# Six products into two PSUM banks: in turn, or three into one and then three into the other

## The chip, the cores and the metric

The kernel runs on one core of a Trainium2 chip. The metric is device time in microseconds (us) of one execution. The runs of the kernel before took 2927.8, 2927.21 and 2923.53 us; their median is 2927.21 us. One more execution was profiled. It took 2925.64 us and its span, from the first to the last instruction, is 2923.9 us.

## The reference

The input `x` is 8 x 3072 x 256 in float32. Three things follow one another:

```python
X = np.fft.fft(np.fft.fft(x, axis=1), axis=2).real      # 24576 rows of 256
h = X @ w_in                                            # first layer, 256 -> 2048
y = (h - np.tanh(h)) @ w_out                            # its second product, 2048 -> 256
h2 = y @ w_in2                                          # second layer, 256 -> 1024
solu = h2 * softmax(h2)
out = layernorm(solu) * g_ln @ w_out2                   # 1024 -> 256
```

## The kernel before

The Fourier transform along the sequence comes first, in some 200 us, and leaves its result in DRAM. The transform along the features is folded into `w_in`. The rest of the run is one long loop over 48 blocks of 512 rows each, and in each block over 16 chunks `m` of 128 hidden features: 768 steps. What one step does on each engine:

- `ab` (L714 to L724) multiplies the step's part of `w_in` with the block's rows: six products of 256 columns on TensorE, into one PSUM bank.
- `lead` and `act_in` (L727 to L749): three VectorE operations make the hidden features h, and ScalarE takes their tanh.
- `act_out` (L752 to L763) forms g = h - tanh(h) on VectorE and splits it in two numbers of reduced precision (float32r), so that products lose nothing that matters: ScalarE rounds g to its high part (L152), and GpSimd then subtracts that from g and leaves the low part (L155). Both stand in one tile `gh`, of which there are three.
- `o1` (L765 to L795) is the second product of the first layer. It multiplies this step's `gh` with 128 rows of `w_out`, which are split in the same way. Three products make one: high by high, low weights by high `gh`, high weights by low `gh`. The 256 outputs are two halves `mt` of 128, each with a PSUM bank of its own (`x2_0` and `x2_1`, one buffer each), so a step has six products of 512 columns here. Over the 16 steps of a block, both banks add up. After the last one (`m == NM - 1`) ScalarE copies both banks to `x2f`, rounds them to `x2s`, and GpSimd makes their low parts.
- `layer2` (L919 to L944) does the second layer for the four groups of 128 rows of a block, spread over the steps in quarters: `h2` (six products of 512 columns into one bank, L806), `expo`, `soft`, `square`, `turn` (a transposition by way of DRAM, which SyncE's queue carries), `split_moved` (high and low parts `ut`, on ScalarE and GpSimd), and `outp` (twelve products of 256 columns, L896).

Nothing reorders the work: every engine runs its instructions in the order in which the program issues them (the schedule is written by hand), and waits at semaphores for the others. The main loop (L949 on) sets this order. In each step TensorE gets `ab`, then one product of the second layer or none, then `o1` of two steps before (four before, in the first block), then again one product of the second layer or none. GpSimd gets, in the order of issue, the low part of `gh` of the step before, the second layer's small operations and the low parts of `ut`, and after a block's last `o1` the low parts of `x2s`.

The order within `o1` is that of two loops, the outer over the three pairs of parts, the inner over the two banks:

```python
for i, (hw, hg) in enumerate(((0, 0), (1, 0), (0, 1))):   # part of the weights, part of gh
    for mt in range(2):                                   # bank
        nc.tensor.matmul(x2p[n][mt], wo1[c][:, hw, k, mt * P : (mt + 1) * P], gh[:, hg], ...)
```

So the six products go to banks 0, 1, 0, 1, 0, 1, and the first four read the high part of `gh`, the last two its low part.

Of the kernel before, what the change touches and what calls it, by code (L numbers as in the profile page):

```python
# [127 lines left out]
def fft2_moe_moe_kernel(  # L128
# [22 lines left out]
    def rnd(o, i):  # L151
        nc.scalar.activation(out=o, in_=i, func=AF.Copy)  # L152

    def rest(eng, o, i, hi):
        eng.tensor_tensor(out=o, in0=i, in1=hi.bitcast(F32), op=ALU.subtract)  # L155
# [609 lines left out]
    def o1(n, m):  # L765
        if m == 0:
            x2p[n] = [p_x2.tile([P, 2 * GP], F32, tag=f"x2_{mt}", name=f"x2p{n}_{mt}") for mt in range(2)]
        gh = gs.pop((n, m))
        c, k = divmod(m, 4)

        for i, (hw, hg) in enumerate(((0, 0), (1, 0), (0, 1))):
            for mt in range(2):
                nc.tensor.matmul(  # L773
                    x2p[n][mt],
                    wo1[c][:, hw, k, mt * P : (mt + 1) * P],
                    gh[:, hg],
                    start=(m == 0 and i == 0),
                    stop=(m == NM - 1 and i == 2),
                )
        if m == NM - 1:  # L780
            xs = wk.tile([P, 2, 2, 2 * GP], F32R, tag="x2s", name=f"x2s{n}")
            x2s[n] = xs
            if n == NG - 1:
                for mt, p in enumerate(x2p.pop(n)):
                    rnd(xs[:, 0, mt], p)
                    rest(nc.vector, xs[:, 1, mt], p, xs[:, 0, mt])
                return
            xf = wk.tile([P, 2, 2 * GP], F32, tag="stage", name=f"x2f{n}")
            for mt, p in enumerate(x2p.pop(n)):
                rnd(xf[:, mt], p)  # L790
            for mt in range(2):
                rnd(xs[:, 0, mt], xf[:, mt])
                rest(nc.gpsimd, xs[:, 1, mt], xf[:, mt], xs[:, 0, mt])
# [155 lines left out]
    for step in range(steps + 2):  # L949
# [13 lines left out]
        for s in (range(o1_done, min(s1 + 1, steps))):  # L963
            o1(*divmod(s, NM))
# [115 lines left out]
```

## Time and profile before

| | |
|---|---|
| median of three runs | 2927.21 us |
| profiled execution | 2925.64 us |
| its span | 2923.9 us |
| TensorE busy | 2881.3 us (99%) |
| VectorE busy | 2403.0 us (82%) |
| GpSimd busy | 1965.2 us (67%) |
| ScalarE busy | 1803.9 us (62%) |
| mean granted TensorE clock | 0.997 |
| HBM traffic | 103 GB/s over the span |

PE is TensorE's stream of products (MATMUL) and PEld its stream of weight loads (LDWEIGHTS), which runs beside it: each product has one load. DVE is VectorE, ACT is ScalarE, POOL is GpSimd. A row of a group of instructions names the line, the engine, the operation, output and inputs, their shapes and the count. A line can be that of a helper: L152 is every rounding on ScalarE, and L155 every subtraction that leaves a low part, so the tile's name tells which one it is. The starts of successive products lie closer together than their durations, because they are pipelined: what a product costs TensorE is read from start to start.

### The profile page before, as it was taken

What the parts mean: (1) busy time and instruction counts of PE and PEld (TensorE: products, weight loads), DVE (VectorE), ACT (ScalarE), POOL (GpSimd) and SP (SyncE); (2) the same over time, 40 slices, a digit from 0 to 9 for tenths busy, and PEclk for the clock granted to TensorE, in tenths of its full rate; (3) what the DMA queues carried; (4) which work ended last, traced back from release to release, by engine and by line L of the source; (5) the groups of instructions that cost most, each with busy time, mean ns of one, the idle gap of its engine ahead of it and who ended that gap; (6) DMA issues with size and microseconds to landing.
All of it is one profiled execution on the core that took longest, in us unless ns stands there. A gap on an engine that the chain in (4) does not pass through costs nothing. (4 is left out here: it accounts for less than half of the span.)

```text
span 2923.9 us, 49792 instructions
## 1 busy us (share of the span) xinstructions
PE 2881.3 (99%) x16799; PEld 2482.3 (85%) x16799; DVE 2403.0 (82%) x4818; ACT 1803.9 (62%) x3287; POOL 1965.2 (67%) x2413
## 2 busy tenths in 40 slices
PE   7899999999999999999999999999999999999999
PEld 3467888888888888888888888888888888888888
DVE  7897888888888888888888888888888888888885
ACT  2345666666666666666666666666666666666665
POOL 0156767777677776777777767777677766777763
PEclk9999999999999999999999999999999999999999
DMA  8781333343334334344334433443434443443331
GB/s 306 252 298 31 88 94 94 90 94 92 87 94 98 89 89 99 88 94 93 89 95 91 96 89 90 97 91 90 94 92 92 93 92 88 95 98 89 89 91 42
DMA packets 876512, 303.75 MB, mean 104 GB/s; under 512 B 788520, under 2 KB 837688, under 8 KB 872960
## 3 DMA queue, kind: packets, MB, share of 16 engines
q1 hardware_dynamic: 873536, 293.95, 40.9%
q10 hardware_dynamic: 2304, 6.29, 0.5%
q8 instruction: 132, 2.16, 0.3%
q14 instruction: 124, 1.02, 0.1%
q0 software_dynamic: 416, 0.33, 0.0%
HBM read 162.01 MB, written 138.47 MB: 103 GB/s over the span
## 5 line engine op out<-in xcount | busy, mean ns | idle before, releaser
L155 POOL TENSOR_TENSOR gh<-g,gh 128x512 fp32r<-128x512 f32 x768 | 993.2, 1297 | 469.3 <-ACT gh L152 469.3
L773 PE MATMUL x2p<-gh,wo 128*128 128x512 f32 x4608 | 1206.5, 397 | 3.6 <-POOL gh L155 2.3
L773 PEld LDWEIGHTS x2p<-gh,wo 128*128 128x128 f32 x4608 | 825.5, 189 | 166.3 <-POOL gh L155 10.7
L749 ACT ACTIVATE t<-h 128x512 f32<-128x512 f32 x768 | 459.5, 598 | 547.8 <-DVE h L743 446.3
L720 PEld LDWEIGHTS ab<-zs,wt 128*128 128x128 f32 x4608 | 649.0, 188 | 72.5 <-DVE h L743 2.7
L720 PE MATMUL ab<-zs,wt 128*128 128x256 f32 x4608 | 668.0, 280 | 2.1 <-DVE h L743 2.1
L754 DVE TENSOR_TENSOR g<-h,t 128x512 f32<-128x512 f32 x768 | 521.8, 679 | 172.0 <-ACT t L749 168.5
L152 ACT ACTIVATE gh<-g 128x512 fp32r<-128x512 f32 x768 | 480.9, 626 | 235.5 <-DVE g L754 223.1
L896 PE MATMUL po<-wo,ut 128*128 128x256 f32 x4608 | 597.8, 278 | 4.4 <-ACT ut L152 2.6
L806 PE MATMUL ph<-wi,x2s 128*128 128x512 f32 x2304 | 597.1, 394 | 0.0
L896 PEld LDWEIGHTS po<-wo,ut 128*128 128x128 f32 x4608 | 560.7, 188 | 10.1 <-POOL ut L155 5.0
L727 DVE SCALAR_TENSOR_TENSOR asb<-nb,wnu,ab 128x256 f32<-128x256 f32 x768 | 367.1, 478 | 221.1 <-PE ab L720 219.3
L806 PEld LDWEIGHTS ph<-wi,x2s 128*128 128x128 f32 x2304 | 420.0, 188 | 84.5
L155 POOL TENSOR_TENSOR ut<-um,ut 128x512 fp32r<-128x512 f32 x372 | 480.8, 1292 | 0.8 <-issue 0.8
L743 DVE TENSOR_TENSOR h<-asb,ab 128x256 f32<-128x256 f32 x768 | 328.8, 428 | 26.5
L742 DVE TENSOR_TENSOR h<-asb,ab 128x256 f32<-128x256 f32 x768 | 329.1, 429 | 26.2
L819 ACT ACTIVATE e<-ph,st 128x1024 f32<-128x1024 f32 x192 | 214.3, 1116 | 97.9 <-DVE st L817 82.1
L817 DVE TENSOR_REDUCE st<-ph 128x1 f32<-128x1024 f32 x192 | 233.6, 1216 | 3.5 <-PE ph L806 3.5
L825 DVE SCALAR_TENSOR_TENSOR u<-ph,e 128x1024 f32<-128x1024 f32 x192 | 233.6, 1217 | 0.0
L152 ACT ACTIVATE ut<-um 128x512 fp32r<-128x512 f32 x372 | 231.1, 621 | 0.0
L856 DVE STREAM_TRANSPOSE tb<-u 128x1024 f32<-128x1024 f32 x186 | 230.0, 1236 | 0.0
L836 ACT ACTIVATE e<-u,st 128x1024 f32<-128x1024 f32 x192 | 219.5, 1143 | 0.0
(101 smaller groups left out, 1531.2 us busy)
## 6 DMA issues: line engine op xcount, KB each, us to landing
mv_d<-tb SPq DMA_DIRECT2D x186, 512.0 KB, 2.6
um<-mv_d SPq DMA_DIRECT2D x744, 128.0 KB, 3.8
out<-o SPq DMA_DIRECT2D x192, 128.0 KB, 1.7
x<-xr SPq DMA_DIRECT2D x23, 1024.0 KB, 7.6
z_d<-zt SPq DMA_DIRECT2D x16, 384.0 KB, 7.4
z_d<-zt ACTq DMA_DIRECT2D x16, 384.0 KB, 6.6
wo<-w_out SPq DMA_DIRECT2D x24, 256.0 KB, 5.5
zf<-z_d SPq DMA_DIRECT2D x48, 128.0 KB, 3.3
```

The costliest lines, as they stand in the source:

```text
L152: nc.scalar.activation(out=o, in_=i, func=AF.Copy)
L155: eng.tensor_tensor(out=o, in0=i, in1=hi.bitcast(F32), op=ALU.subtract)
L720: nc.tensor.matmul(pab[:, u], wt[c][:, hw, u, o : o + P], zs[:, hz, u], start=(i == 0), stop=(i == 2))
L727: nc.vector.scalar_tensor_tensor(out=asb, in0=zg[n][1], scalar=wnu[:, m : m + 1], in1=pab[:, 0], op0=ALU.mult, op1=ALU.add)
L742: nc.vector.tensor_tensor(out=h[:, 0], in0=asb, in1=pab[:, 1], op=ALU.add)
L743: nc.vector.tensor_tensor(out=h[:, 1], in0=asb, in1=pab[:, 1], op=ALU.subtract)
L749: nc.scalar.activation(out=t, in_=h, func=AF.Tanh)
L754: nc.vector.tensor_tensor(out=g, in0=hs.pop((n, m)).rearrange("p u n -> p (u n)"), in1=ts_.pop((n, m)).rearrange("p u n -> p (u n)"), op=A ...
L773: nc.tensor.matmul(x2p[n][mt], wo1[c][:, hw, k, mt * P : (mt + 1) * P], gh[:, hg], start=(m == 0 and i == 0), stop=(m == NM - 1 and i == 2),)
L806: nc.tensor.matmul(ph[:, fs], xs[:, hx, k, tk], wi2[:, hw, k, fs], start=(k == 0 and q == 0), stop=(k == 1 and q == 2),)
L817: nc.vector.tensor_reduce(out=st[:, 0:1], in_=ph, axis=AX.X, op=ALU.max, negate=True)
L896: nc.tensor.matmul(po[:, :D], ut[:, hu, ks], wo2[:, hw, k], start=(k == 0 and q == 0), stop=(k == NK2 - 1 and q == 2),)
```

## The change

The two loops of `o1` change places. Each product keeps its operands and its bank, and each bank still gets its three products in the same order. The banks now come as 0, 0, 0, 1, 1, 1. The parts of `gh` are read as high, high, low, high, high, low, where they were read as high four times and then low twice. The weight loads follow their products.

```diff
@@ -768,8 +768,8 @@
         gh = gs.pop((n, m))
         c, k = divmod(m, 4)
 
-        for i, (hw, hg) in enumerate(((0, 0), (1, 0), (0, 1))):
-            for mt in range(2):
+        for mt in range(2):
+            for i, (hw, hg) in enumerate(((0, 0), (1, 0), (0, 1))):
                 nc.tensor.matmul(
                     x2p[n][mt],
                     wo1[c][:, hw, k, mt * P : (mt + 1) * P],
```

## Rows read from the trace of the kernel before

**Rows 1.** The page: span, busy time of PE, and PE's granted clock in 40 slices.

```profile
span 2923.9 us, 49792 instructions
...
PE 2881.3 (99%) x16799; PEld 2482.3 (85%) x16799; DVE 2403.0 (82%) x4818; ACT 1803.9 (62%) x3287; POOL 1965.2 (67%) x2413
...
PEclk9999999999999999999999999999999999999999
```

**Rows 2.** Windows of two blocks: busy us (count) of PE, PEld, DVE, ACT, POOL; clock; DMA.

```profile
588.16:644.30 56.14, 56.14 (x338) 49.51 (x337) 45.98 (x93) 36.14 (x66) 41.26 (x53) 1.00 0.39 92
644.30:700.20 55.90, 55.90 (x339) 49.44 (x338) 46.08 (x93) 36.25 (x66) 39.55 (x49) 1.00 0.39 92
```

**Rows 3.** Timeline of PE in an ordinary stretch: start us, length us, what.

```profile
1503.78 0.87 PE L720 MATMUL ab<-zs,wt 128*128 128x256 f32 x6
1504.48 1.56 PE L806 MATMUL ph<-wi,x2s 128*128 128x512 f32 x6
1505.88 1.57 PE L773 MATMUL x2p<-gh,wo 128*128 128x512 f32 x6
1507.28 0.87 PE L720 MATMUL ab<-zs,wt 128*128 128x256 f32 x6
1507.98 1.54 PE L896 MATMUL po<-wo,ut 128*128 128x256 f32 x12
1509.36 1.56 PE L773 MATMUL x2p<-gh,wo 128*128 128x512 f32 x6
```

**Rows 4.** Groups by line: count, busy us, mean ns, idle before and releasers.

```profile
L773 PE MATMUL x2p<-gh,wo 128*128 128x512 f32 x4608 | 1206.5, 397 | 3.6 <-POOL gh L155 2.3 <-ACT gh L152 0.6 <-ACT x2f L152 0.5
...
L896 PE MATMUL po<-wo,ut 128*128 128x256 f32 x4608 | 597.8, 278 | 4.4 <-ACT ut L152 2.6 <-POOL ut L155 1.2 <-DVE ut L155 0.7
```

**Rows 5.** Timeline of POOL across the border of two blocks, 636 to 645 us.

```profile
636.02 0.19 POOL L844 TENSOR_TENSOR st<-st 128x1 f32<-128x1 f32 x1 [1.08 <-ACT e L836]
...
637.39 1.29 POOL L155 TENSOR_TENSOR ut<-um,ut 128x512 fp32r<-128x512 f32 x1
638.64 1.30 POOL L155 TENSOR_TENSOR gh<-g,gh 128x512 fp32r<-128x512 f32 x1
639.90 1.29 POOL L155 TENSOR_TENSOR ut<-um,ut 128x512 fp32r<-128x512 f32 x1
641.15 2.55 POOL L155 TENSOR_TENSOR x2s<-x2f,x2s 128x512 fp32r<-128x512 f32 x2
643.65 2.55 POOL L155 TENSOR_TENSOR gh<-g,gh 128x512 fp32r<-128x512 f32 x2
```

**Rows 6.** Timeline of PE over the same border and the next two o1.

```profile
637.33 1.57 PE L773 MATMUL x2p<-gh,wo 128*128 128x512 f32 x6
...
644.30 1.56 PE L773 MATMUL x2p<-gh,wo 128*128 128x512 f32 x6
...
646.41 1.56 PE L773 MATMUL x2p<-gh,wo 128*128 128x512 f32 x6
```

**Rows 7.** Timeline of POOL, PEld and PE behind the border at 1484 us.

```profile
1484.38 1.31 POOL L155 TENSOR_TENSOR gh<-g,gh 128x512 fp32r<-128x512 f32 x1
...
1484.71 0.77 PEld L773 LDWEIGHTS x2p<-gh,wo 128*128 128x128 f32 x4
1485.74 0.30 PEld L773 LDWEIGHTS x2p<-gh,wo 128*128 128x128 f32 x2 [0.26 <-POOL gh L155]
...
1484.83 1.65 PE L773 MATMUL x2p<-gh,wo 128*128 128x512 f32 x6
```

**Rows 8.** The same behind the border at 1092 us: POOL and PE.

```profile
1092.20 1.30 POOL L155 TENSOR_TENSOR gh<-g,gh 128x512 fp32r<-128x512 f32 x1
...
1092.36 1.92 PE L773 MATMUL x2p<-gh,wo 128*128 128x512 f32 x6
```

**Rows 9.** Waits of PEld, 300 to 2840 us, then 200 to 300: us, times, longest.

```profile
PEld x2p L773 <- POOL gh L155: 4.6, 17, 0.5
...
PEld x2p L773 <- POOL gh L155: 6.1, 9, 1.1
```

**Rows 10.** POOL and PE behind the borders at 307 us and at 2718 us.

```profile
306.97 1.30 POOL L155 TENSOR_TENSOR gh<-g,gh 128x512 fp32r<-128x512 f32 x1
...
307.61 0.86 PE L773 MATMUL x2p<-gh,wo 128*128 128x512 f32 x3
...
2717.78 1.31 POOL L155 TENSOR_TENSOR gh<-g,gh 128x512 fp32r<-128x512 f32 x1
...
2718.45 0.86 PE L773 MATMUL x2p<-gh,wo 128*128 128x512 f32 x3
```

**Rows 11.** Timeline of ACT over the border of Rows 5.

```profile
638.07 0.62 ACT L152 ACTIVATE ut<-um 128x512 fp32r<-128x512 f32 x1
638.70 1.09 ACT L152 ACTIVATE x2f<-x2p 128x512 f32<-128x512 f32 x2
639.67 1.15 ACT L152 ACTIVATE x2s<-x2f 128x512 fp32r<-128x512 f32 x2
```

**Rows 12.** Group of POOL by line, 300 to 2840 us; its idle time before stands last.

```profile
L155 POOL TENSOR_TENSOR x2s<-x2f,x2s 128x512 fp32r<-128x512 f32 x92 | 117.6, 1305 | 0.0
```

## The prediction

> **What bounds the kernel now.** I read the page first: PE is busy for 2881.3 us of a span of 2923.9 us, at a granted clock of nine tenths or more (the level of 2.4 GHz) in all 40 slices [rows 1]. Next, windows of whole blocks: over 56.14 and 55.90 us PE has no gap at all, while POOL, the next one that matters here, is busy for some 40 us [rows 2]. So in the loop nearly every nanosecond that TensorE loses or saves is a nanosecond of the kernel. Then the timeline of PE gives the price of each kind of work, from start to start: six products of `o1` 1.40 us (1505.88 to 1507.28), six of `h2` 1.40 (1504.48 to 1505.88), six of `ab` 0.70, twelve of `outp` 1.38 [rows 3]. A product of `o1` thus takes 1.40 / 6 = 0.233 us, and the six start at 0, 0.23, 0.47, 0.70, 0.93 and 1.17 us after the first.
>
> What matters next is when POOL has the low part of `gh` ready, which the last two products read. The groups by line say that PE as a whole hardly waits for it, 2.3 us in the run [rows 4]. That total hides how near it is. At the border of two blocks POOL runs without a pause from 636.02 us: the second layer's small operations, a `ut`, a `gh`, a `ut`, both `x2s` of the block that has ended, and only then, at 643.65, the low parts of two `gh`, the first of which is that of chunk m = 1 [rows 5]. At half of 2.55 us and a little, as the single ones take 1.30, it ends at 644.95. TensorE begins the `o1` of m = 1 at 644.30 [rows 6]: the low part comes 0.65 us into the six products. The fifth product, at 0.93, doesn't feel it. The third, at 0.47, would.
>
> **The change part by part.**
>
> *Number and kind of instructions.* Nothing is added or removed: 4608 products of 512 columns and as many weight loads stay. In both orders no two neighbours share their weights, so no load falls away. No DMA is moved, and no queue but TensorE's is passed.
>
> *The wait.* The first reader of the low part moves from fifth to third place, 2 x 0.233 = 0.467 us earlier. What waits is the weight load of the product: behind the border at 1484 us PEld has issued four loads, idles, and issues the last two at 1485.74, when POOL (1484.38 + 1.31 = 1485.69) is through [rows 7]. Behind the waiting one stand all the rest of `o1`, then `ab` of the next step; and for that `ab` wait DVE, ACT and POOL.
>
> What a late low part costs is read from two groups that are already late. At 1484 us it ends 0.86 us into the group, and the group is 1.65 long instead of 1.56: 0.09 lost [rows 7]. At 1092 us it ends 1092.20 + 1.30 - 1092.36 = 1.14 into it, and the group is 1.92 long: 0.36 lost [rows 8]. Both say the same: the loss begins when the low part ends later than 0.775 us into the group, that is 0.155 before the fifth product's turn, and from there it is one for one. Moved to the third product, the limit is 0.467 - 0.155 = 0.31 us.
>
> Now the sum, by kinds of block. From 300 to 2840 us PEld waits for POOL's `gh` 17 times, 4.6 us in total [rows 9]; these are borders as at 1484 us, already beyond 0.775, and each loses the whole shift more: 17 x 0.467 = 7.9 us. In the same stretch lie the borders into 46 blocks (2 to 47), so 29 are as at 644 us and lose nothing today; the first and the last of them have the low part at 0.66 and 0.64 [rows 10]. Each would lose 0.65 - 0.31 = 0.335: 29 x 0.335 = 9.7 us. If the whole idle time of the weight loads counted (0.467 for each), it would be 13.5; if only what exceeds the product's own turn (0.65 - 0.47 = 0.18), 5.3. I take the middle value, since the two late groups give it. In the first two blocks, 200 to 300 us, PEld waits nine times, 6.1 us in all [rows 9]. There POOL sets the pace, so a wait that begins earlier mostly moves the wait that follows: between one shift, 0.5, and nine, 4.2; I take 1.4, three.
>
> Other steps keep their margin. The next tightest of a block is m = 2: its low part is the second at 643.65 and ends at 646.20 [rows 5], its `o1` starts at 646.41 [rows 6], so it ends before the group begins, while the limit is 0.31 after.
>
> A stall isn't given back. What the POOL chain starts from is ACT's square at 636.02 [rows 5], which follows TensorE's products of the steps before; a TensorE that is later by 0.335 us starts the next block's chain later by as much, and meets the same stall at the next border.
>
> *The pace.* Does a product run faster or slower if the one before it went into the same bank? `h2` puts six in a row into one bank and takes 1.40, as `o1` does in turn; `ab` stays in one bank and takes 0.70 or 0.71 for half the columns, 1.42 for as many; `outp`, twelve of 256 columns into one bank, 1.38 [rows 3]. So a group of `o1` may come out 0.02 shorter or longer, times 768 groups: 15.4 us to either side. I take nought, as the row of the same shape has.
>
> *The earlier end of bank 0.* Its last product of a block moves from fifth to third. ACT can't use this: it ends a `ut` at 638.69 and begins `x2f` at 638.70 [rows 11], when the fifth of the six products from 637.33 has been through either way. I take nought. The other end is a gain of all that the borders and the shift would lose, as the POOL chain could move up by 0.467 us at most; it is worked out as the first rival. The Trainium skill ("Perfetto Trace Analysis", section "Optimizing Tensor Performance") speaks for that rival: it wants independent groups of products in different banks, so that the eviction of one overlaps the products of the next, and the new order does let bank 0 be read while bank 1 gets its three. By that rule the change would bring something here; the rows of ACT say that it can't.
>
> Sum: 7.9 + 9.7 + 1.4 = 19.0 us on the profiled execution's 2925.64 (its span and 1.7 us around it): 2944.6 us. The median of the runs shown is 1.6 us above this execution, so against it the same sum gives 2946.2. I say 2945.
>
> **The rivals.**
>
> *Bank 0's eviction starts the POOL chain earlier, and nothing changes.* If POOL's `x2s` waited for that eviction, they and the `gh` behind them would move up by as much as 0.467 us; the low part would end at 0.18, before 0.31 (at the 17 late borders at 0.39, for a loss of 0.08, about today's), and only the start's 1.4 us would remain: 2927 us. Against it: all 92 `x2s` on POOL from 300 to 2840 us have 0.0 us of idle time before them [rows 12]; in the border shown ACT begins both roundings at 639.67 [rows 11] and POOL is not free for their low parts until 641.15 [rows 5].
>
> *One bank at a time is the faster way to add (not slower).* Place: all 768 groups. If a group ran at the pace inside `outp`, (1.54 - 0.28) / 11 = 0.1145 for 256 columns [rows 3, 4], it would last 12 x 0.1145 = 1.374 and save 20 us, which eats the stalls up: 2925 us. It decides from 19.0 / 768 = 0.025 us in a group. Against it: `h2` and `ab`, in one bank too, run at 1.40 and 1.42. For it: `o1` is the only group that alternates, and none is faster than `outp`.
>
> *POOL falls behind at more borders.* If a stalled TensorE reorders who is late, and all 46 borders lose the whole 0.467, it is 46 x 0.467 + 1.4 = 22.9: 2949 us. For it: some borders lie at 0.65 and some at 0.86, so POOL's place does vary by 0.2. Against it: within each kind it repeats.
>
> *The wait stays where it is*, because the program's wait is laid on another instruction than the first reader: nothing moves, 2926 us. Against it: it sits on the fifth product's load today [rows 7].
>
> **How the numbers follow.** Forecast with its pace bounds, 0.80; POOL later at more borders, 0.07; eviction earlier, 0.05; faster pace, 0.05; wait unmoved, 0.03. The likeliest is 2945. Its own uncertainty is the loss at a border (14.6 to 22.8 with the bounds above, around 19.0) and the pace; half of the pace's bounds, 8 us, on either side covers most of it: 2935 to 2954. That leaves out the cases near 2926 and the tail of pace, some 2 in 10. A measurement of this kernel can tell 0.2%, 5.9 us. Slower by over that: forecast and late POOL, nearly whole, 0.86. Within it: most of the eviction, of the wait unmoved, and half of the faster pace, 0.10. Faster: the rest of the faster pace, 0.04.
>
> **What would show it.** Right: behind 46 borders PEld issues two loads of `o1`, idles for POOL's `gh`, and the group of m = 1 lasts about 1.56 + 0.335 = 1.9 us (2.1 at the late ones); waits of PEld for that tile appear some 46 times instead of 17; groups elsewhere stay at 1.40 from start to start; a block is 56.4 us long instead of 56.1. Wrong: groups of m = 1 at 1.56 (no stall), or all groups of `o1` at 1.38 or 1.42 (the pace), or `x2f` well before the `ut` that precedes it in order.

## The result, and the profile after

The changed kernel took 2943.95 us (median of four runs, 2942.42 to 2945.44); the kernel before, beside it, 2925.82 (2923.53 to 2927.8). The medians differ by 18.1 us, a ratio of 1.0062; the estimate over all runs is 1.0066, with a 95% interval of 1.0053 to 1.0078. So the change made the kernel slower. The forecast was 2945, in a range of 2935 to 2954.

The page of the changed kernel, the lines that answer to [rows 1]:

```profile
span 2942.9 us, 49792 instructions
...
PE 2892.8 (98%) x16799; PEld 2480.7 (84%) x16799; DVE 2407.0 (82%) x4818; ACT 1800.7 (61%) x3287; POOL 1964.7 (67%) x2413
...
PEclk9999999999999999999999999999999999999999
```

As many instructions, the same granted clock, and PE busy for 11.5 us more, of the 19.0 us by which the span grew. That is a trap of this view: the products are the same. In a steady stream their records overlap; at a stall they overlap less, and the one that waited has a longer record (below), so that much of a stall counts as busy. The idle time of TensorE's loads shows the stall. The waits of PEld in the changed kernel, 300 to 2840 us (total us, times, longest), answer to the first line of [rows 9]:

```profile
PEld x2p L773 <- POOL gh L155: 26.8, 46, 1.0
PEld po L896 <- POOL ut L155: 3.5, 17, 0.5
```

There were 17 such waits for `gh`, of 4.6 us, and now there are 46. Of these, 45 stand at m = 1, one behind every border of two blocks in this stretch; the border into the last block now lies at 2849 us, just outside it, and waits too. The 46th is another step, m = 9 of block 36 (PEld):

```profile
2256.44 0.30 PEld L773 LDWEIGHTS x2p<-gh,wo 128*128 128x128 f32 x2
2257.14 0.77 PEld L773 LDWEIGHTS x2p<-gh,wo 128*128 128x128 f32 x4 [0.40 <-POOL gh L155]
```

A border whose low part ends some 0.65 us into the group is called early here, one of the 17 that stalled before is called late. An early border, to be laid beside [rows 5, 6], in the timelines of POOL, PEld and PE of the changed kernel:

```profile
645.53 2.54 POOL L155 TENSOR_TENSOR x2s<-x2f,x2s 128x512 fp32r<-128x512 f32 x2
648.04 1.28 POOL L155 TENSOR_TENSOR gh<-g,gh 128x512 fp32r<-128x512 f32 x1
...
648.56 0.30 PEld L773 LDWEIGHTS x2p<-gh,wo 128*128 128x128 f32 x2
649.37 0.77 PEld L773 LDWEIGHTS x2p<-gh,wo 128*128 128x128 f32 x4 [0.51 <-POOL gh L155]
...
648.68 1.90 PE L773 MATMUL x2p<-gh,wo 128*128 128x512 f32 x6
650.42 0.86 PE L720 MATMUL ab<-zs,wt 128*128 128x256 f32 x6
```

The low part ends at 649.32, still 0.64 into the group. PEld has issued two loads where it had issued four, and holds the last four until 649.37. None passes the waiting one, though the fourth and fifth need nothing from POOL. The group is 1.90 us long, where it was 1.56; from its start to that of `ab` it is 1.74 instead of 1.40. Narrower windows of the same timeline show the second, third and fourth product alone:

```profile
648.91 0.40 PE L773 MATMUL x2p<-gh,wo 128*128 128x512 f32 x1
...
649.38 0.50 PE L773 MATMUL x2p<-gh,wo 128*128 128x512 f32 x1
...
649.71 0.40 PE L773 MATMUL x2p<-gh,wo 128*128 128x512 f32 x1
```

The third starts with its own load (649.37), where in a steady stream the loads run ahead of the products (1484.71 against 1484.83 in [rows 7]). Its record is 0.50 long instead of 0.40, and the fourth starts 0.33 behind it instead of 0.23. So a late low part costs 0.05 from its end to the load, and 0.10 more, as these rows suggest, for a load that nothing hides: together about the 0.155 us that the prediction read from two groups without naming their cause. PE stands idle for only 0.07 us of all this.

A late border, which answers to [rows 7] (PEld, then PE):

```profile
1494.67 0.30 PEld L773 LDWEIGHTS x2p<-gh,wo 128*128 128x128 f32 x2
1495.68 0.77 PEld L773 LDWEIGHTS x2p<-gh,wo 128*128 128x128 f32 x4 [0.70 <-POOL gh L155]
...
1494.79 0.63 PE L773 MATMUL x2p<-gh,wo 128*128 128x512 f32 x2
1495.69 1.20 PE L773 MATMUL x2p<-gh,wo 128*128 128x512 f32 x4 [0.27 <-POOL gh L155]
1496.73 0.86 PE L720 MATMUL ab<-zs,wt 128*128 128x256 f32 x6
```

This one takes 1.94 from start to start, 0.54 over 1.40, where it lost 0.09 before. Over all 46 borders, read in the timelines of both kernels, the low part ends as late as before within 0.03 us. The 29 early groups take 1.732 us on average instead of 1.403, the 17 late ones 1.965 instead of 1.496: 17.5 us together.

The other groups kept their pace. In an ordinary stretch of the changed kernel, answering to [rows 3]:

```profile
1500.91 1.56 PE L806 MATMUL ph<-wi,x2s 128*128 128x512 f32 x6
1502.31 1.57 PE L773 MATMUL x2p<-gh,wo 128*128 128x512 f32 x6
1503.72 0.87 PE L720 MATMUL ab<-zs,wt 128*128 128x256 f32 x6
```

Six products of `o1` take 1.41 us here and six of `h2` 1.40, as before within the last digit. Whole blocks, answering to [rows 2] (busy us and count of PE, PEld, DVE, ACT, POOL; clock; DMA):

```profile
592.23:648.68 56.45, 56.39 (x339) 49.41 (x337) 46.09 (x93) 36.06 (x66) 41.22 (x53) 1.00 0.40 92
648.68:704.90 56.22, 56.15 (x339) 49.35 (x337) 46.18 (x93) 36.17 (x66) 39.58 (x49) 1.00 0.39 92
```

They last 0.31 and 0.32 us longer than the same two before, each about the price of one early border.

What the earlier end of bank 0 does is seen where a block ends, in the timelines of PE and ACT that answer to [rows 6, 11]:

```profile
641.70 1.57 PE L773 MATMUL x2p<-gh,wo 128*128 128x512 f32 x6
...
642.44 0.62 ACT L152 ACTIVATE ut<-um 128x512 fp32r<-128x512 f32 x1
642.96 1.08 ACT L152 ACTIVATE x2f<-x2p 128x512 f32<-128x512 f32 x2
643.92 1.16 ACT L152 ACTIVATE x2s<-x2f 128x512 fp32r<-128x512 f32 x2
```

ACT begins `x2f` 1.26 us into the six products, where it began 1.37 into them before (638.70 - 637.33): 0.11 earlier. POOL still begins `x2s` only at 645.53, right behind its `ut`.

### The profile page after: what moved, and what is told of

The parts are those of the page before. It is cut to its first block, busy times and chain, and to the rows that moved or that the text cites. A ratio compares the mean times of both kernels' runs of the same rounds, so it can differ in the third digit from the quotient of the medians.

```text
span 2942.9 us, 49792 instructions
## 1 busy us (share of the span) xinstructions
PE 2892.8 (98%) x16799; PEld 2480.7 (84%) x16799; DVE 2407.0 (82%) x4818; ACT 1800.7 (61%) x3287; POOL 1964.7 (67%) x2413
```

## The experiments

Each ratio is to the kernel before, run beside it on the same chip (medians 2923.91, 2924.95 and 2923.62 us in the three sets).

**Low part third, banks in turn.** It parts the wait from the order of the banks. Against the kernel before:

```diff
-        for i, (hw, hg) in enumerate(((0, 0), (1, 0), (0, 1))):
+        for i, (hw, hg) in enumerate(((0, 0), (0, 1), (1, 0))):
             for mt in range(2):
```

> The banks stay in turn (0, 1, 0, 1, 0, 1) as in the kernel before, but the pairs come as high-high, high weights by low gh, low weights by high gh, so that the low part of gh is first read by the third product. If the wait for POOL's low part is the cause, this loses what the change lost, about 18 us: 2944 us, with PEld waiting for POOL's gh behind all 46 borders. If the cause were three products in a row into one bank (the accumulation, or the pace), nothing is lost: 2926 us.

Measured: 2941.59 us, ratio 1.0062 (1.0047 to 1.0077). The waits of PEld, 300 to 2840 us:

```profile
PEld x2p L773 <- POOL gh L155: 26.5, 46, 1.0
```

The whole loss comes back with the banks still in turn.

**Low part fifth, banks nearly one by one.** Against the changed kernel, the call of the product left out:

```diff
-        for mt in range(2):
-            for i, (hw, hg) in enumerate(((0, 0), (1, 0), (0, 1))):
...
+        parts = ((0, 0), (1, 0), (0, 1))
+        order = ((1, 0), (1, 1), (0, 0), (0, 1), (0, 2), (1, 2))
+        for mt, i in order:
+            hw, hg = parts[i]
...
```

> The banks come as 1, 1, 0, 0, 0, 1, so that the products of a bank follow one another but for the last, and the low part of gh is first read by the fifth product, as in the kernel before. If the wait is the cause: 2926 us, no different from before, and 17 waits of PEld for POOL's gh from 300 to 2840 us. If it is the same bank twice or three times in a row, of which there are three neighbours here against four in the change and none before: three quarters of the loss, about 2939 us.

Measured: 2923.75 us, ratio 1.0000 (0.9991 to 1.0010). The same view:

```profile
PEld x2p L775 <- POOL gh L155: 4.7, 17, 0.5
```

Three of five neighbouring products share a bank here, and nothing is lost or gained. Together the two runs settle it: what counts is the place of the first reader of the low part, not the order of the banks.

**Only m = 1, and all but m = 1.** Where in the block the loss arises. The first kernel against the changed one, the call of the product left out; the second has the two lists of `order` exchanged:

```diff
-        for mt in range(2):
-            for i, (hw, hg) in enumerate(((0, 0), (1, 0), (0, 1))):
...
+        parts = ((0, 0), (1, 0), (0, 1))
+        order = [(mt, i) for mt in range(2) for i in range(3)] if m == 1 else [(mt, i) for i in range(3) for mt in range(2)]
+        for mt, i in order:
+            hw, hg = parts[i]
...
```

> Bank by bank only in chunk m = 1 of each block, in turn in the fifteen others. If the loss is the wait at the border of two blocks, it is nearly all here: 46 borders, 17.6 us, and some 0.5 us of the start: 2943 to 2944 us. If the new order cost something in every group of o1, one sixteenth is left: 2927 us.

> The reverse: bank by bank in every chunk but m = 1, which stays in turn. If the loss is the wait at the borders, only the start's share is left, 0.5 to 1.5 us: 2926 to 2928 us, and this is the purest measure of the order's pace, nought by my rows. If the new order costs in every group: 15 of 16 parts, 2943 us.

Measured: with m = 1 alone 2940.91 us, ratio 1.0059 (1.0042 to 1.0076); with all the others 2925.53 us, ratio 1.0007 (0.9998 to 1.0016). So 48 of 768 groups hold 17.0 of some 18 us, and the other 720 together 1.6, which the interval doesn't part from nought. A pace of 0.02 us in a group, the bound that I had kept, would have been 14.4 us in those 720: it is excluded.

**Low part second.** If the wait is the cause, its price must grow with the shift. Against the changed kernel:

```diff
         for mt in range(2):
-            for i, (hw, hg) in enumerate(((0, 0), (1, 0), (0, 1))):
+            for i, (hw, hg) in enumerate(((0, 0), (0, 1), (1, 0))):
```

> Bank by bank as in the change, but each bank takes high-high, then high weights by low gh, then low weights by high gh: the low part is first read by the second product, 0.233 us earlier than in the change. If the wait is the cause, each of the 46 borders loses that much more, 10.7 us, and the start about 1: 2944 + 11.5 = 2955 us. If the loss were that of three products in a row into one bank, it is that of the change: 2944 us.

Measured: 2954.39 us, ratio 1.0101 (1.0086 to 1.0116), 29.4 us above before; the change was 18.1 above, so the second shift cost 11.3. At the 46 borders the timelines show 10.7 of it. One thing in its trace I hadn't foreseen (waits of PEld, 300 to 2840 us):

```profile
PEld x2p L773 <- POOL gh L155: 36.0, 66, 1.1
PEld po L896 <- POOL ut L155: 0.6, 2, 0.3
```

There are 66 waits for `gh`, not 46, and the waits of `outp` for `ut` have all but gone (17 of 3.5 us in the changed kernel). The 20 new ones stand at m = 9, as the one of block 36 did already. In every block POOL splits rows of the next one there, and in 21 blocks it has two operations more to do for that (L233); in these, `gh` ends some 0.22 us into the group (0.53 in block 36). This is such a group, 1.73 long instead of 1.56 (timeline of PE):

```profile
902.49 1.73 PE L773 MATMUL x2p<-gh,wo 128*128 128x512 f32 x6
```

In the same 21 blocks `outp` used to wait behind m = 11 for a `ut` that POOL delivers at its own time; TensorE, already late from m = 9, now finds it ready. From the `o1` of m = 9 to that of m = 13 these blocks take 14.25 us on average in the changed kernel and 14.26 here: a stall is given back by the next one. At the borders it isn't.

**POOL's x2s one step later.** Takes away what makes the border's `gh` late: the two low parts of `x2s`, which POOL had ahead of it. The same edit, shortened to its main lines, was made to the changed kernel and to the kernel before:

```diff
             for mt in range(2):
                 rnd(xs[:, 0, mt], xf[:, mt])
-                rest(nc.gpsimd, xs[:, 1, mt], xf[:, mt], xs[:, 0, mt])
+                lows.append((xs[:, 1, mt], xf[:, mt], xs[:, 0, mt]))
...
         out_done = max(out_done, min(step - lag + 1, steps))
+        for low in lows:
+            rest(nc.gpsimd, *low)
+        lows.clear()
```

> The changed kernel, but POOL makes the two low parts of x2s one step later, behind the low part of gh of m = 1 instead of ahead of it. By the POOL chain at the border, that gh then ends about 2.5 us earlier, before its o1 begins, and that of m = 2 stays where it is, at the border of its own limit (it ends 0.2 us before its group). If POOL's place is the cause of the stall: the 17.6 us of the borders go, and with them the 1.6 us that late borders cost in the kernel before: 2925 to 2928 us. If the stall had another cause than what POOL has ahead of it: 2944 us.

> The kernel before with the same move of POOL's two low parts of x2s. By the chain it loses the 1.6 us of its 17 late borders and nothing else: 2924 us, just below before and within what can be told. If POOL's later x2s make h2 wait for them, it is slower: one wait of up to 1 us for each of 46 blocks, up to 2970 us.

Measured: on the changed kernel 2922.34 us, ratio 0.9992 (0.9982 to 1.0001); on the kernel before 2922.67, ratio 0.9992 (0.9983 to 1.0002). The timelines of POOL and PE, of the first of the two, at the border of [rows 5]:

```profile
638.34 1.29 POOL L155 TENSOR_TENSOR gh<-g,gh 128x512 fp32r<-128x512 f32 x1
639.59 2.55 POOL L155 TENSOR_TENSOR x2s<-x2f,x2s 128x512 fp32r<-128x512 f32 x2
642.10 1.30 POOL L155 TENSOR_TENSOR gh<-g,gh 128x512 fp32r<-128x512 f32 x1
...
641.35 1.56 PE L774 MATMUL x2p<-gh,wo 128*128 128x512 f32 x6
```

The `gh` of m = 1 ends at 639.63, 1.7 us before its group begins, and the group is 1.56 long. With its cause gone, the order of the products no longer matters: the two orders are 0.3 us apart. `h2` doesn't wait for the later `x2s`.

A second measurement with more executions, to see whether this beats both kernels:

> The changed kernel with POOL's x2s one step later, measured in more rounds: by the trace of its first run no border stalls, so 2 us below the kernel before, 2922 us; if that was the spread of the runs, 2925 us.

Measured: 2922.28 us, ratio 0.9996 (0.9987 to 1.0005). It beats the changed kernel; that it beats the kernel before isn't shown.

**The row split earlier.** An attempt at the waits of `outp`, with the banks in turn and `x2s` later. Against the kernel with both:

```diff
-        if 1 <= n and n + 1 < NG and j in (9, 11):
+        if 1 <= n and n + 1 < NG and j in (9, 10):
             split_z(n + 1, int(j > 9))
```

The second kernel has `j in (8, 10)` and `int(j > 8)`.

> The banks in turn and POOL's x2s one step later, and besides, the second half of the next block's row split (split_z: on POOL, and a rounding on ACT) in step 10 of a block where it was in step 11. In 21 of 46 blocks outp waits behind m = 11 for POOL's low part of ut, 5 to 6 us of TensorE in all; in those blocks POOL and ACT have just split rows. If the split is what delays them: 2923 less 5, 2918 us. If ut is late for another reason: 2923 us. If the split in step 10 delays gh there: slower.

> The same with the halves of the row split in steps 8 and 10, so that two steps stand between them as before. Same expectations: 2918 us if the split in step 11 delays ut; 2923 us if not.

Measured: 2933.02 us, ratio 1.0031 (1.0020 to 1.0043), and 2934.12 us, ratio 1.0035 (1.0022 to 1.0047): both slower. For the first I had named that as the third case, for the second not at all. The only line of PEld's waits in the first, 300 to 2840 us:

```profile
PEld x2p L774 <- POOL gh L155: 16.3, 21, 0.8
```

POOL now has the split ahead of the `gh` of m = 10, and in the 21 blocks `o1` waits for that, longer than `outp` had waited; the second kernel waits in them at m = 8 and at m = 10, 42 times, 22.7 us. It is the mechanism of the change once more: not what POOL does, but what it has ahead of a product's operand.

The waits for `ut` are gone, but not because `ut` comes sooner. Block 23 shows it, in the timelines of PE and POOL of the first kernel, and then of the kernel before (where the `o1` of m = 8 starts at 1509.36 [rows 3]):

```profile
1512.20 1.56 PE L774 MATMUL x2p<-gh,wo 128*128 128x512 f32 x6
...
1519.36 0.73 PE L774 MATMUL x2p<-gh,wo 128*128 128x512 f32 x2 [0.35 <-POOL gh L155]
...
1525.53 1.54 PE L897 MATMUL po<-wo,ut 128*128 128x256 f32 x12
...
1523.81 1.29 POOL L155 TENSOR_TENSOR ut<-um,ut 128x512 fp32r<-128x512 f32 x1
```

```profile
1521.96 1.77 PE L896 MATMUL po<-wo,ut 128*128 128x256 f32 x12
...
1520.95 1.30 POOL L155 TENSOR_TENSOR ut<-um,ut 128x512 fp32r<-128x512 f32 x1
```

Counted from the start of the `o1` of m = 8, `ut` ends at 12.90 here and at 12.89 before, while TensorE comes to `outp` at 13.33 instead of 12.60. So the stall at m = 10 swallowed the wait for `ut`, as the one at m = 9 did above. That the split makes `ut` late isn't shown by these runs; it stays likely, as in the blocks without the two operations of L233 `ut` ends some 0.95 us sooner.

## Why the prediction was right

- *The wait moves from fifth to third reader, and is not hidden.* Right: the low part still ends 0.64 us into the group, and PEld holds four loads instead of two.
- *The limit of 0.31 us and one for one behind it.* Right: 0.335 us was forecast for an early border, and the 29 lose 0.329 on average (0.34 at 648.68); a late one was to lose 0.467 more, and the 17 lose 0.469 (0.54 - 0.09 = 0.45 at 1494.79).
- *The sum.* 17.6 us was forecast for the borders. The timelines give 17.5, and with m = 1 alone 17.0 were measured. For the start's share and everything else I had put 1.4. The run with all the others leaves 1.6, between -0.6 and 4.7 by its interval, which tells little. The two timelines are closer: from the first product of `o1` to m = 1 of block 2 the changed kernel takes 0.8 us longer, so this term was some 0.6 too high. That the two profiled spans differ by 19.0, the very sum, is partly chance: the first product of `o1` starts at 205.4 us after and at 204.1 before, and that is the Fourier stage, which the change doesn't touch. In the traces of the other runs it starts between 200.2 and 206.2.
- *The pace.* Taken as nought, right; the bound of 15.4 us on either side was far too wide, since its rows (`ab`, `outp`) differ from `o1` in more than the bank. Groups of `o1` in chunks other than 1, 2 and 9 take 1.4025 us on average from start to start in both kernels, over blocks 2 to 46.
- *Bank 0's eviction.* No gain in time, as forecast, but one of its two reasons was misread. ACT does use the earlier end, by 0.11 us: in [rows 11] `x2f` stood behind the fifth product, not only behind the `ut`. The other reason holds: POOL does the `x2s` at 645.53 right behind its other work, and the stall stays. Only the move of POOL's own order took it away. The rule of the Trainium skill ("Perfetto Trace Analysis", section "Optimizing Tensor Performance"), that one bank's eviction should overlap the products of another, brings nothing here: no run shows a gain from the earlier end of bank 0, not even the one with all chunks but m = 1 in the new order.
- *A stall isn't given back.* Right at the borders. Not quite elsewhere: PEld's waits for `ut` fell from 21 (4.2 us) to 17 (3.5), and in the run with the low part second nearly all of them went.
- *What was wrong:* I named m = 2 as the next tightest chunk. It is m = 9: in 21 blocks its low part ends 0.22 us into the group, 0.09 before the limit, and in block 36 even 0.54. There the change lost another 0.23 us (1.63 from start to start instead of 1.40), which the sum left out; the other 20 cost nothing, and showed at once when the limit moved by another 0.233. So the count of 46 waits came out as forecast partly by luck: it is 45 borders and this one.
- *A row misread:* the 2.3 us that PE waited for `gh` in the kernel before [rows 4] do not hide the borders. All of it falls between 200 and 300 us; from 300 to 2840 PE waits for no `gh` at all, and only the idle time of the loads [rows 9] shows the 17 late borders.

## What to carry to other kernels

A loop order on the engine that bounds the kernel is also an order of first use: ask of each operand that another engine makes last where its first reader stands, and compare that with when it is ready at its latest, not on average. Total waits hide this margin: in the loop of the kernel before, PE showed no wait for `gh` and its loads 4.6 us, for 46 borders of which 17 stalled already and 29 were 0.13 us short of it. And if the producer is the late one, changing what it has ahead of that operand can make the consumer's order harmless, as with `x2s`, or move the stall to another operand, as with the row split.

## What the runs showed that I had not expected

- A stall can be swallowed by the next one: with the low part read second, 20 new waits at m = 9 took the place of the waits behind m = 11 (3.5 us fell to 0.6), at no cost in the whole. So a wait that is gone doesn't show that its cause is gone.
- Moving 0.88 + 0.75 us of POOL's work by one step replaced 3.4 us of idle loads for one operand by 16.3 for another, and made the kernel 9.4 us slower than before.
- How exactly the pace stays, for which I had left 15.4 us: products in a row into one PSUM bank or into two in turn take the same time here; 720 groups in the new order differ from the old by 1.6 us in 2925, within the interval.
